# Where a Strassen sum is kept, where two halves of a weight tile lie, and ScalarE's order between two stages

## The chip, the cores and the metric

The kernel runs on one core of a Trainium2 chip. The metric is the device time of one execution in microseconds. The core's engines work side by side, each through its own list of instructions in order: TensorE (matmul, "PE", its weight loads "PEld"), VectorE ("DVE"), ScalarE ("ACT"), GpSimd ("POOL") and SyncE ("SP", which issues DMAs; GpSimd issues some too). They meet at semaphores: an instruction waits until the work that it depends on has been counted.

## The reference, cut to what matters

```python
def _attn_ref(q, k, v):                       # B=2, H=8, S=1152, D=64
    q_pool = q.reshape(B, H, S // 2, 2, D).mean(axis=3)
    scores = 1.0 / np.sqrt(D) * np.matmul(q_pool, k.transpose(0, 1, 3, 2))
    scores = scores - np.max(scores, axis=-1, keepdims=True)
    attn = np.exp(scores)
    attn = attn / (np.sum(attn, axis=-1, keepdims=True) + 1e-09)
    return np.matmul(attn, v)

def _moe_ref(x, domain_probs, w1, w2):        # x: 1152x512, 4 experts, F=1024
    p = domain_probs / (domain_probs.sum(-1, keepdims=True) + 1e-09)
    out = np.zeros((N, D))
    for e in range(E):
        h = np.maximum(x @ w1[e], 0.0)
        out += p[:, e:e + 1] * (h @ w2[e])
    return out
```

The attention output, as 1152 rows of 8 x 64 columns, is the `x` of the second function. Everything is fp32.

## The kernel before

**Stages.** Attention comes first: 8 pairs of heads, 9 tiles of 128 query rows each, 72 tiles in a row. Then 16 units of the expert layer, unit `u` being a quarter of one expert's hidden columns. Attention's tiles live in a pool `ap` that is closed at the end of the stage; a second pool `mp` lies over the same memory, and the first write to a tile of `mp` waits for the last users of every `ap` tile that it overlaps (`reuse_waits="tile"`). Tiles are laid out in the order in which they are made.

**fp32 in three products.** Each operand is split into a rounded half ("hi", z=0) and a remainder ("lo", z=1), and a product is hi·hi + hi·lo + lo·hi. The rounding is a ScalarE copy. The remainder is made by a subtraction on GpSimd or VectorE (`h_lo`, L715; `split_parts`, L496), or by rounding the negated value and adding the exact one by a DMA that accumulates (`h_add` L718, `w2_add` L742, `w1_add` L760).

**Strassen (Winograd form) in both layers.** One 2x2 block product takes 7 block products. The first layer's are `PRODS` (`mprod`, L139): they accumulate in three pairs of PSUM banks, CX, CY and CZ, and VectorE takes the sums u1, u2, C21, C22 and C12 out of them (`add_part`, L763). Bank pair CY is read three times while it grows: for u1, u2 and C21; in the first unit ScalarE also copies it once, as y7. After the relu these blocks give the operands of the second layer: S1 = C21 + C22 (GpSimd, L779), S2 = C11 - S1 and S3 = C11 - C21 (VectorE, L776), S4 = C12 + S2 (GpSimd `sum_s4`, L782). The second layer's products are P1 to P7 (`pprod`, L814), with weight blocks W and their sums T1 to T4 (`w2_sums`, L750), and VectorE adds them, weighted, into `acc` (L788, L790). `wide` (L826) does the rows left over.

**Where blocks are kept.** `UT` maps names to slots of the tile `xr`; several names share a slot, and the framework makes a write wait for all readers of what lay there. `hs` holds the split second-layer operands, `w2s` the split second-layer weights, for both z in one tile, `w1s` (in `kk`) the first-layer weights, `wf` and `w2f` their raw loads.

**Order.** Nothing is scheduled by a planner: each engine executes its instructions in the order of the code. Units overlap: the loop body for unit `u` interleaves the second layer of `u` with the first layer of `v = u + 1` and the weights of `w = u + 2`. On TensorE a unit is P5, P4, `mprod(v,2)`, `wide`, P3, `mprod(v,6)`, P2, then P1 of the next, `mprod(v,0)`, `mprod(v,1)`, P6, `mprod(v,3)`, P7, `mprod(v,5)`, `mprod(v,4)`. P2, P3 and P5 write CY, the others CO. On GpSimd `h_lo("S4")` stands behind `w1_add(w, 3, 7)`, late in the unit.

**The seam.** Between the last PV product (`PV_part`, L418, with `finish`, L455) and unit 0 the code of L844 to L894 makes the first operands: `w2_hi(0, "W")` and `w1_split(1, 0, 7, 1)` on ScalarE, `a11_hi`, the four roundings in `late` (S2, S1, A22, S4 of the last head pair's columns) with the copy of y7 between them.

Of the kernel before, what the change touches and what calls it, by code (L numbers as in the profile page):

```python
# [8 lines left out]
F32 = mybir.dt.float32  # L9
F32R = mybir.dt.float32r  # L10
# [7 lines left out]
def attention_moe_kernel(ctx, tc, q, k, v, probs, w1, w2, out):  # L18
    nc = tc.nc
    B, H, S, D = q.shape  # L20
    NT, DM = out.shape
    E, _, FF = w1.shape
    P = 128
    HALF = 64
    NPAIR = H // 2
    KT = S // P
# [75 lines left out]
    def flat(t):  # L102
        return t.rearrange("p o k f -> p (o k f)")
# [18 lines left out]
    def load_w2(u):  # L122
        if u < NU:
            e, j = divmod(u, 4)
            nc.sync.dma_start(w2f, w2[e].rearrange("(s j p) d -> j p s d", s=2, p=P)[j])

    UT = {n: xr[:, k, o * HT:(o + 1) * HT] for n, k, o in (
        ("m1", 0, 0), ("u1", 0, 1), ("u2", 2, 0), ("y7", 2, 1), ("C21", 1, 0), ("C22", 1, 1), ("S1", 3, 0), ("C12", 3, 1))}
    UT |= {"S2": UT["y7"], "S3": UT["u2"], "S4": UT["C21"]}
    UV = {n: t.rearrange("p (c x) -> p c x", c=2) for n, t in UT.items()}  # L130

    PRODS = [("X", "A11", "B11"), ("Y", "S2", "T2"), ("X", "A12", "B21"), ("Y", "S3", "T3"),
# [19 lines left out]
    with ExitStack() as actx:  # L152
        ap = actx.enter_context(tc.tile_pool(name="ap", bufs=1))

        vn = [ap.tile([P, 2, KT, D], F32, name=f"vn{i}") for i in range(2)]
        sx = [ap.tile([P, S], F32, name=f"sx{i}") for i in range(3)]
        raw = ap.tile([P, 7 * P], F32, name="raw")
        GW = [256, 320]
        aT = [ap.tile([P, 2, KT, w], F32, name=f"aT{i}") for i, w in enumerate(GW)]
        rb = [ap.tile([P, w], F32, name=f"rb{i}") for i, w in enumerate(GW)]  # L160
        spread = ap.tile([P, 4 * HALF], F32, name="spread")
        mn = [ap.tile([P, 1], F32, name=f"mn{i}") for i in range(3)]
# [246 lines left out]
        def PV_part(n, grp, k0, k1):  # L409
# [4 lines left out]
            po = opt[0]  # L414
            w = GW[grp]
            for kt in range(k0, k1):
# [32 lines left out]
        def finish(n, grp, po):  # L449
            b, hp = pairs[n]  # L450
            w, kt = GW[grp], hp % 2
            c = slice(256 * grp, 256 * grp + w)
# [45 lines left out]
        late = []  # L498
# [90 lines left out]
        for g in range(NTL):  # L589
            n, i = divmod(g, 9)  # L590
# [95 lines left out]

        mp = ctx.enter_context(tc.tile_pool(name="mp", bufs=1, reuse_waits="tile"))
        w2t = mp.tile([P, 4, 256], F32, name="w2t")
        acc = mp.tile([P, NQT, DM], F32, name="acc")
        w2s = mp.tile([P, 2, 12, 256], F32R, name="w2s")  # L690
        hs = mp.tile([P, 2, 61, HALF], F32R, name="hs")

        HS = {"A11": (0, 9), "S1": (10, 8), "A12": (19, 9), "A22": (29, 8), "A21": (10, 8), "S2": (37, 8), "S3": (45, 8), "S4": (53, 8),
# [26 lines left out]
        def rows(t):  # L720
            return t.rearrange("p o f -> p (o f)")

        def wop(u, w, z, n=1):
            o = WT[w] if w[0] == "T" else 4 * (u % 2) + 2 * int(w[1] == "2") + int(w[2] == "2")
            return rows(w2s[:, z, o:o + n])

        def w2_part(u, name):
            if name == "W":
                return [wop(u, "W11", z, 4) for z in range(2)], w2f.rearrange("p s f -> p (s f)")
            a, n = name  # L730
            return [rows(w2s[:, z, 8 + a:8 + a + n]) for z in range(2)], rows(w2t[:, a:a + n])

        def w2_hi(u, name, neg=True):
            if u < NU:
                dst, src = w2_part(u, name)
                for z in range(1 + neg):
                    nc.scalar.activation(dst[z], src, AF.Copy, scale=-1.0 if z else 1.0)

        def w2_add(u, name):
            if u < NU:  # L740
                dst, src = w2_part(u, name)
                nc.gpsimd.dma_start(dst[1].bitcast(F32), src, accum_op=ALU.add)  # L742

        def w2_sums(parts):
            w = {f"W{s + 1}{d + 1}": w2f[:, s, d * 256:(d + 1) * 256] for s in range(2) for d in range(2)}
            w |= {n: w2t[:, o - 8] for n, o in WT.items()}
            for i in parts:
                o, x, y, op = (("T1", "W12", "W11", ALU.subtract), ("T2", "T1", "W22", ALU.subtract),
                               ("T3", "W22", "W12", ALU.subtract), ("T4", "W21", "T2", ALU.add))[i]
                nc.gpsimd.tensor_tensor(w[o], w[x], w[y], op)  # L750

        def w1_split(u, a, b, z0=0):
            if u < NU:
                for z in range(z0, 2):
                    nc.scalar.activation(
                        flat(w1s[u % 2][:, z, a:b]), flat(wf[:, a:b]), AF.Copy, scale=-1.0 if z else 1.0)

        def w1_add(u, a, b):
            if u < NU:
                nc.gpsimd.dma_start(flat(w1s[u % 2][:, 1, a:b]).bitcast(F32), flat(wf[:, a:b]), accum_op=ALU.add)  # L760
# [48 lines left out]
        def pprod(u, name, chain=CO):  # L809
            op, w, b, d, first = PR2[name]  # L810
            pc = [chain[:, i // 2, (i % 2) * 256:(i % 2) * 256 + 256] for i in range(4)]
            for i in range(4):
                for m, (x, y) in enumerate(TERMS):
                    nc.tensor.matmul(pc[i], cols(op, x, 2 * i), wop(u, w, y),  # L814
                                     start=(first == 1 and m == 0 and i % 2 == 0), stop=(m == 2), skip_group_check=True)
                for t in range(i - 1, i + 1) if i % 2 else ():
                    gated(u, 4 * b + t, 256 * d, 256 * d + 256, pc[t])

        def wide(u, idx, pc, c0=0, c1=DM):
            for sl in range(2):  # L820
                if idx == 8:
                    op, o = (("A11", 8), ("A12", 8))[sl]
                else:
                    op, o = (("A11", "A12"), ("A21", "A22"))[idx // 4][sl], 2 * (idx % 4)
                for m, (x, y) in enumerate(TERMS):
                    nc.tensor.matmul(pc, cols(op, x, o), wop(u, f"W{sl + 1}1", y, 2)[:, c0:c1],  # L826
                                     start=(sl + m == 0), stop=(sl + m == 3), skip_group_check=True)
            gated(u, idx, c0, c1, pc)
            if u == NU - 1:
                store(idx, c0, c1)  # L830
# [4 lines left out]
        def mprod(u, p, kts=(0, 1)):  # L835
            n = PRODS[p][0]
            for kt in kts:
                product(u, p, kt, chains[n], (u, n) not in begun)
            begun.add((u, n))

        def copy_m1():
            nc.scalar.activation(UV["m1"], CX[:, :, :CW], AF.Copy)

        w2_hi(0, "W")  # L844
        w2_sums((0, 1))
        w2_add(0, "W")
        w2_sums((2, 3))
        load_w2(1)
        w1_split(1, 0, 7, 1)
        w1_add(1, 0, 7)  # L850
        load_w1(2)
        a11_hi()
        begun.add((0, "X"))
        mprod(0, 3)
        for p in late[:2]:
            p[0]()
        nc.scalar.activation(UV["y7"], CY[:, :, :CW], AF.Copy)  # L857
        mprod(0, 4, (0,))
        for p in late[2:]:
            p[0]()  # L860
        mprod(0, 1, (0,))
        for p in late:
# [1 line left out]
        mprod(0, 1, (1,))  # L864
        w2_hi(0, (0, 4), False)
        w2t_lo, w2t_src = w2_part(0, (0, 4))
        for c in range(2):
            cs = slice(c * 512, (c + 1) * 512)
# [148 lines left out]
```

## Time and profile before

| | us |
|---|---|
| median of 3 runs (638.51 to 639.1) | 638.57 |
| the profiled execution | 639.26 |
| its span | 637.5 |
| TensorE busy | 599.0 (94%) |
| weight loads busy | 530.7 (83%) |
| VectorE busy | 458.8 (72%) |
| GpSimd busy | 423.3 (66%) |
| ScalarE busy | 399.1 (63%) |

Attention runs to about 236 us in the span, the units from there to the end. In a timeline each line is a run of equal instructions: when the first began, how long until the last ended, engine, source line, operation, what it writes and reads, how many, and in brackets how long the engine had been idle before and which instruction ended that. Matmuls overlap a little, and their ends are modelled. Idle time of an engine costs nothing by itself; it matters where another engine waits for what comes late.

### The profile page before, as it was taken

The numbers are of one execution on the slowest core, as the hardware profiler recorded it, in microseconds if no ns is written. First come the engines' busy times: TensorE is split into PE (matmuls) and PEld (weight loads), VectorE is DVE, ScalarE is ACT, GpSimd is POOL, SyncE is SP. The second block draws the span as 40 slices with busy tenths as digits, with TensorE's granted clock in tenths as the row PEclk, the third lists the DMA queues.
The fourth block names the chain that finished last, engine by engine and source line by source line (L and its number), as shares of the span: only waits on it lengthen the run. The fifth ranks groups of instructions, "written<-read, shape, count | busy, mean of one in ns | idle before, by whom it ended". The sixth has DMA issues, their size and how long they took to land. (4 is left out here: it accounts for less than half of the span.)

```text
span 637.5 us, 14430 instructions
## 1 busy us (share of the span) xinstructions
PE 599.0 (94%) x5585; PEld 530.7 (83%) x5585; DVE 458.8 (72%) x903; ACT 399.1 (63%) x611; POOL 423.3 (66%) x534
## 2 busy tenths in 40 slices
PE   7999999999999998699999999999999999999997
PEld 6777777777777768598998988988988988988996
DVE  6778878777777765477677686786776776776774
ACT  5766777767767747556566666656756746746630
POOL 4746536455454966777977977977877977877620
PEclk9999999999999998899999999999999999999999
DMA  4877466484744207749569669579578587587415
GB/s 149 195 209 197 113 161 138 124 200 126 174 100 113 67 2 156 132 112 212 101 133 195 121 136 204 106 146 191 108 156 174 113 169 146 133 178 135 97 34 149
DMA packets 54180, 89.38 MB, mean 140 GB/s; under 512 B 4704, under 2 KB 28640, under 8 KB 54112
## 3 DMA queue, kind: packets, MB, share of 16 engines
q0 software_dynamic: 12672, 38.34, 34.0%
q1 hardware_dynamic: 40560, 48.94, 28.4%
q10 hardware_dynamic: 880, 1.18, 0.5%
q8 instruction: 44, 0.72, 0.5%
q14 instruction: 24, 0.20, 0.1%
HBM read 30.97 MB, written 2.36 MB: 52 GB/s over the span
## 5 line engine op out<-in xcount | busy, mean ns | idle before, releaser
L790 DVE SCALAR_TENSOR_TENSOR acc<-banks,pw,acc 128x256 f32<-128x256 f32 (+2 forms) x429 | 182.1, 488 | 13.9 <-PE banks L826 7.0
L814 PE MATMUL banks<-w2s,hs 128*128 128x256 f32 x1260 | 166.9, 286 | 24.8 <-DVE xr L763 24.8
L814 PEld LDWEIGHTS banks<-w2s,hs 128*128 128x128 f32 x1260 | 159.7, 193 | 29.7 <-DVE xr L763 28.2
L383 DVE TENSOR_SCALAR_CACHE_REDUCE sx<-banks 128x1152 f32<-128x1152 f32 x72 | 97.7, 1357 | 42.2 <-PE banks L372 19.1
L763 DVE TENSOR_TENSOR xr<-banks,xr 128x576 f32<-128x576 f32 x79 | 58.4, 754 | 90.0 <-POOL hs L715 44.3
L715 POOL TENSOR_TENSOR hs<-xr,hs 128x512 fp32r<-128x512 f32 (+2 forms) x79 | 95.9, 1232 | 25.4 <-ACT hs L712 13.8
L389 ACT ACTIVATE sx<-sx,mn 128x1152 f32<-128x1152 f32 x72 | 90.6, 1258 | 19.9 <-DVE sx L383 19.8
L766 ACT ACTIVATE xr<-xr 128x576 f32<-128x576 f32 x48 | 32.7, 681 | 106.8 <-DVE xr L763 106.8
L712 ACT ACTIVATE hs<-xr 128x512 fp32r<-128x512 f32 (+3 forms) x109 | 76.0, 725 | 21.2 <-DVE xr L776 18.7
L418 PE MATMUL banks<-aT,vn 128*64 128x320 f32 (+1 forms) x576 | 85.5, 418 | 0.0
L139 PE MATMUL banks<-xb,kk 128*128 128x288 f32 x480 | 77.5, 297 | 3.3 <-ACT xr L857 3.0
L139 PE MATMUL banks<-q2all,kk 128*128 128x288 f32 x448 | 76.1, 299 | 0.0
L139 PEld LDWEIGHTS banks<-xb,kk 128*128 128x128 f32 x480 | 68.5, 191 | 4.2 <-ACT xr L857 3.2
L405 ACT ACTIVATE aT<-banks 128x640 f32<-128x640 f32 x72 | 50.5, 702 | 30.4 <-PE banks L215 30.2
L139 PEld LDWEIGHTS banks<-q2all,kk 128*128 128x128 f32 x448 | 65.5, 191 | 0.0
L372 PEld LDWEIGHTS banks<-kk,q2all 64*128 64x128 f32 x504 | 54.5, 186 | 12.0 <-DVE sx L383 6.1
L372 PE MATMUL banks<-kk,q2all 64*128 64x512 f32 (+1 forms) x504 | 63.2, 365 | 0.5 <-DVE sx L383 0.5
L215 PEld LDWEIGHTS banks<-ident,sx 64*128 64x128 f32 x1296 | 54.4, 139 | 6.2 <-issue 2.7
L215 PE MATMUL banks<-ident,sx 64*128 64x64 f32 x1296 | 57.9, 225 | 1.3 <-ACT raw L238 0.5
L139 PE MATMUL banks<-xa,kk 128*128 128x288 f32 x384 | 56.9, 297 | 0.0
L742 POOL DMA_DIRECT2D w2s<-w2t x28 | 26.1, 933 | 46.1 <-issue 43.9
L98 POOL TENSOR_TENSOR kq<-kq 128x256 f32<-128x256 f32 x64 | 50.8, 870 | 6.4 <-DMA kq<-in_moe_w_dram 5.2
(120 smaller groups left out, 865.7 us busy)
## 6 DMA issues: line engine op xcount, KB each, us to landing
hs<-xr POOLq DMA_DIRECT2D x15, 576.0 KB, 4.9
kq<-in_moe_w_dram SPq DMA_DIRECT2D x64, 128.0 KB, 5.8
qsf<-in_moe_w_dram SPq DMA_DIRECT2D x16, 512.0 KB, 6.2
w2s<-qsf POOLq DMA_DIRECT2D x16, 512.0 KB, 5.0
q2all<-q2all SPq DMA_DIRECT2D x28, 256.0 KB, 4.1
kk<-kq POOLq DMA_DIRECT2D x14, 512.0 KB, 6.8
w2s<-w2t POOLq DMA_DIRECT2D x28, 256.0 KB, 4.9
kk<-kq POOLq DMA_DIRECT2D x14, 384.0 KB, 4.2
```

The lines of the kernel that those rows point to most:

```text
L98: nc.gpsimd.tensor_tensor(g(o), g(a), g(b), ALU.subtract)
L139: nc.tensor.matmul(chain[:, c, :CW], w1s[u % 2][:, a, WI[wo], kt, :], xop(xo, z, kt)[:, c * CW:(c + 1) * CW], start=(first and kt == 0 and ...
L215: nc.tensor.transpose(pt[:, a, j, :], src[r], ident[r, r])
L372: mm = nc.tensor.matmul(sp[:, cs[c]], q2[n % 2][r, zq, h, ts_], src[n % 2][r, zk, cs[c]], start=(zq + zk == 0), stop=(zq == 1), skip_group ...
L383: nc.vector.tensor_scalar(sx[g % 3].rearrange("p (c x) -> p c x", c=3), spt.pop(g), -INV, None, ALU.mult, ALU.min, accum_out=mn[g % 3])
L389: nc.scalar.activation(sx[g % 3], sx[g % 3], AF.Exp, bias=mn[g % 3], scale=-1.0, accum_out=sums[n % 2][:, i:i + 1])
L418: nc.tensor.matmul(po[h * HALF:(h + 1) * HALF, :w], vn[n % 2][:, h, kt, :], aT[grp][:, h, kt, :], start=(kt == 0), stop=(kt == KT - 1))
L712: nc.scalar.activation(hop(op, z), raw_of(op), AF.Copy, scale=-1.0 if z else 1.0)
L715: nc.gpsimd.tensor_tensor(hop(op, 1), raw_of(op), hop(op, 0).bitcast(F32), ALU.subtract)
L763: nc.vector.tensor_tensor(UV[name], chain[:, :, :CW], UV[part], ALU.add)
L790: nc.vector.scalar_tensor_tensor(ac, src, pw[:, idx, e:e + 1], ac, ALU.mult, ALU.add)
L814: nc.tensor.matmul(pc[i], cols(op, x, 2 * i), wop(u, w, y), start=(first == 1 and m == 0 and i % 2 == 0), stop=(m == 2), skip_group_check= ...
```

## The change

Three edits. S4 is formed in the slot of S2 (`y7`'s), in place, and no longer in the slot of C21. The split second-layer weights `w2s` become two tiles, `w2s0` (hi) and `w2s1` (lo), made before `acc`, and the order of attention's tiles in memory is changed: by their sizes `w2s0` lies over `vn0`, `sx0`, `sx1` and `raw`, `w2s1` over `raw`, `sx2` and `aT0`, `acc` over `aT0` and `aT1`, `hs` over `aT1`, `vn1`, `rb0`, `rb1` and the small tiles behind them. Before, `w2s` lay over `sx2`, `raw`, `aT0` and the start of `aT1`. At the seam `w1_split(1, 0, 7, 1)` goes ahead of `w2_hi(0, "W")` on ScalarE, and one rounding of `late`, not two, goes ahead of the copy of y7.

```diff
--- before.py
+++ after.py
@@ -126,7 +126,7 @@
 
     UT = {n: xr[:, k, o * HT:(o + 1) * HT] for n, k, o in (
         ("m1", 0, 0), ("u1", 0, 1), ("u2", 2, 0), ("y7", 2, 1), ("C21", 1, 0), ("C22", 1, 1), ("S1", 3, 0), ("C12", 3, 1))}
-    UT |= {"S2": UT["y7"], "S3": UT["u2"], "S4": UT["C21"]}
+    UT |= {"S2": UT["y7"], "S3": UT["u2"], "S4": UT["y7"]}
     UV = {n: t.rearrange("p (c x) -> p c x", c=2) for n, t in UT.items()}
 
     PRODS = [("X", "A11", "B11"), ("Y", "S2", "T2"), ("X", "A12", "B21"), ("Y", "S3", "T3"),
@@ -152,11 +152,13 @@
     with ExitStack() as actx:
         ap = actx.enter_context(tc.tile_pool(name="ap", bufs=1))
 
-        vn = [ap.tile([P, 2, KT, D], F32, name=f"vn{i}") for i in range(2)]
-        sx = [ap.tile([P, S], F32, name=f"sx{i}") for i in range(3)]
+        GW = [256, 320]
+        vn = [ap.tile([P, 2, KT, D], F32, name="vn0")]
+        sx = [ap.tile([P, S], F32, name=f"sx{i}") for i in range(2)]
         raw = ap.tile([P, 7 * P], F32, name="raw")
-        GW = [256, 320]
+        sx.append(ap.tile([P, S], F32, name="sx2"))
         aT = [ap.tile([P, 2, KT, w], F32, name=f"aT{i}") for i, w in enumerate(GW)]
+        vn.append(ap.tile([P, 2, KT, D], F32, name="vn1"))
         rb = [ap.tile([P, w], F32, name=f"rb{i}") for i, w in enumerate(GW)]
         spread = ap.tile([P, 4 * HALF], F32, name="spread")
         mn = [ap.tile([P, 1], F32, name=f"mn{i}") for i in range(3)]
@@ -686,8 +688,8 @@
 
         mp = ctx.enter_context(tc.tile_pool(name="mp", bufs=1, reuse_waits="tile"))
         w2t = mp.tile([P, 4, 256], F32, name="w2t")
+        w2s = [mp.tile([P, 12, 256], F32R, name=f"w2s{z}") for z in range(2)]
         acc = mp.tile([P, NQT, DM], F32, name="acc")
-        w2s = mp.tile([P, 2, 12, 256], F32R, name="w2s")
         hs = mp.tile([P, 2, 61, HALF], F32R, name="hs")
 
         HS = {"A11": (0, 9), "S1": (10, 8), "A12": (19, 9), "A22": (29, 8), "A21": (10, 8), "S2": (37, 8), "S3": (45, 8), "S4": (53, 8),
@@ -722,13 +724,13 @@
 
         def wop(u, w, z, n=1):
             o = WT[w] if w[0] == "T" else 4 * (u % 2) + 2 * int(w[1] == "2") + int(w[2] == "2")
-            return rows(w2s[:, z, o:o + n])
+            return rows(w2s[z][:, o:o + n])
 
         def w2_part(u, name):
             if name == "W":
                 return [wop(u, "W11", z, 4) for z in range(2)], w2f.rearrange("p s f -> p (s f)")
             a, n = name
-            return [rows(w2s[:, z, 8 + a:8 + a + n]) for z in range(2)], rows(w2t[:, a:a + n])
+            return [rows(w2s[z][:, 8 + a:8 + a + n]) for z in range(2)], rows(w2t[:, a:a + n])
 
         def w2_hi(u, name, neg=True):
             if u < NU:
@@ -841,22 +843,22 @@
         def copy_m1():
             nc.scalar.activation(UV["m1"], CX[:, :, :CW], AF.Copy)
 
+        w1_split(1, 0, 7, 1)
         w2_hi(0, "W")
         w2_sums((0, 1))
         w2_add(0, "W")
         w2_sums((2, 3))
         load_w2(1)
-        w1_split(1, 0, 7, 1)
         w1_add(1, 0, 7)
         load_w1(2)
         a11_hi()
         begun.add((0, "X"))
         mprod(0, 3)
-        for p in late[:2]:
+        for p in late[:1]:
             p[0]()
         nc.scalar.activation(UV["y7"], CY[:, :, :CW], AF.Copy)
         mprod(0, 4, (0,))
-        for p in late[2:]:
+        for p in late[1:]:
             p[0]()
         mprod(0, 1, (0,))
         for p in late:
```

The engines' lists differ in ScalarE's at the seam alone; elsewhere only waits and the tile names do. Below stands ScalarE's list at the seam before, each row with the semaphores that it waits for (`w2s<-qsf` is `w2_hi(0, "W")`, `kk_75<-kq` is `w1_split`, `hs<-banks` is `a11_hi`, `q2all<-xr` are the roundings of `late`, `xr<-banks` is the copy of y7).

```order
L737 ACTIVATE w2s<-qsf 128x1024 [waits DMAHW4_49,PE_49,Activation_49]
L737 ACTIVATE w2s<-qsf 128x1024
L755 ACTIVATE kk_75<-kq 128x1792 [waits DMAHW5_49,DMAHW6_49,DMAHW3_49,DMAHW7_49,DMAHW0_49,Pool_49]
L769 ACTIVATE hs<-banks 128x576 [waits DVE_49,Pool_49]
L495 ACTIVATE q2all<-xr 128x320 [waits DVE_49] x2
L857 ACTIVATE xr<-banks 128x576 [waits PE_49]
L495 ACTIVATE q2all<-xr 128x320
L495 ACTIVATE q2all<-xr 128x320 [waits DVE_49]
L737 ACTIVATE w2s<-w2t 128x1024 [waits Pool_49]
```

And the same place now (`w2s_3456` is `w2s0`, `w2s_3457` is `w2s1`).

```order
L757 ACTIVATE kk_75<-kq 128x1792 [waits DMAHW5_49,DMAHW4_49,DMAHW6_49,DMAHW3_49,DMAHW7_49,DMAHW0_49,Pool_49]
L739 ACTIVATE w2s_3456<-qsf 128x1024 [waits DMAHW4_49,Activation_49]
L739 ACTIVATE w2s_3457<-qsf 128x1024 [waits PE_49,Activation_49]
L771 ACTIVATE hs<-banks 128x576 [waits DVE_49,DMAHW3_49,Activation_49,Pool_49]
L497 ACTIVATE q2all<-xr 128x320 [waits DVE_49]
L859 ACTIVATE xr<-banks 128x576 [waits PE_49]
L497 ACTIVATE q2all<-xr 128x320 [waits DVE_49]
L497 ACTIVATE q2all<-xr 128x320
L497 ACTIVATE q2all<-xr 128x320 [waits DVE_49]
L739 ACTIVATE w2s_3456<-w2t 128x1024 [waits Pool_49]
```

The split of w1 stands first, the first rounding of W has lost its wait for TensorE (the second has one, for the PV products that read `aT0`), and the copy of y7 is the second row behind `a11_hi`, not the third.

VectorE's list has the same instructions in the same order. Before, at the place in a middle unit where P7's last sums (L790) are followed by C21 (the first L763), C22 (the second) and P5's first sum:

```order
L790 SCALAR_TENSOR_TENSOR acc<-banks,pw,acc 128x256 [waits PE_49]
L790 SCALAR_TENSOR_TENSOR acc<-banks,pw,acc 128x256
L763 TENSOR_TENSOR xr<-banks,xr 128x576 [waits PE_49,Activation_49,Pool_49]
L763 TENSOR_TENSOR xr<-banks,xr 128x576 [waits DVE_49,PE_49]
L790 SCALAR_TENSOR_TENSOR acc<-banks,pw,acc 128x256 [waits DVE_49,PE_49]
```

Now:

```order
L792 SCALAR_TENSOR_TENSOR acc<-banks,pw,acc 128x256 [waits PE_49]
L792 SCALAR_TENSOR_TENSOR acc<-banks,pw,acc 128x256
L765 TENSOR_TENSOR xr<-banks,xr 128x576 [waits PE_49,Pool_49]
L765 TENSOR_TENSOR xr<-banks,xr 128x576 [waits DVE_49,PE_49,Pool_49]
L792 SCALAR_TENSOR_TENSOR acc<-banks,pw,acc 128x256 [waits DVE_49,PE_49]
```

C21's row has lost its wait for ScalarE (`h_hi("S4")`) and keeps one for GpSimd; C22's row has one for GpSimd that it did not have.

## Rows read from the trace of the kernel before

**Rows 1.** The page, slices of the span; granted TensorE clock in tenths.

```profile
PEclk9999999999999998899999999999999999999999
```

**Rows 2.** Waits of the whole span: who waited for whom; us, times, longest.

```profile
PEld banks L814 <- DVE xr L763: 28.2, 14, 6.0
PE banks L814 <- DVE xr L763: 24.8, 14, 5.8
```

**Rows 3.** Timeline, TensorE, a middle unit; start, us, work, [idle before].

```profile
441.04 3.14 PE L814 MATMUL banks<-w2s,hs 128*128 128x256 f32 x24 [1.46 <-DVE xr L763]
...
450.02 3.04 PE L814 MATMUL banks<-w2s,hs 128*128 128x256 f32 x24
...
462.95 0.96 PE L139 MATMUL banks<-q2all,kk 128*128 128x288 f32 x6
465.37 3.14 PE L814 MATMUL banks<-w2s,hs 128*128 128x256 f32 x24 [1.46 <-DVE xr L763]
```

**Rows 4.** Timeline, TensorE's weight loads, the same unit.

```profile
465.37 2.81 PEld L814 LDWEIGHTS banks<-w2s,hs 128*128 128x128 f32 x23 [1.70 <-DVE xr L763]
```

**Rows 5.** Timeline, VectorE, the same unit.

```profile
445.89 1.42 DVE L776 SCALAR_TENSOR_TENSOR xr<-banks,xr 128x576 f32<-128x576 f32 x2 [0.61 <-PE banks L139]
...
448.77 1.65 DVE L790 SCALAR_TENSOR_TENSOR acc<-banks,pw,acc 128x256 f32<-128x256 f32 x4
...
464.56 1.42 DVE L763 TENSOR_TENSOR xr<-banks,xr 128x576 f32<-128x576 f32 x2 [2.86 <-POOL hs L715]
```

**Rows 6.** Timeline, GpSimd, the same unit.

```profile
443.88 1.74 POOL L779 TENSOR_TENSOR xr<-xr 128x576 f32<-128x576 f32 x1
...
447.40 4.24 POOL L715 TENSOR_TENSOR hs<-xr,hs 128x512 fp32r<-128x512 f32 x4 [0.94 <-DVE xr L776]
...
462.66 1.87 POOL L715 TENSOR_TENSOR hs<-xr,hs 128x512 fp32r<-128x512 f32 x1
```

**Rows 7.** Timeline, TensorE, the seam and unit 0.

```profile
242.08 1.06 PE L139 MATMUL banks<-xb,kk 128*128 128x288 f32 x6 [2.95 <-ACT xr L857]
...
249.27 1.60 PE L814 MATMUL banks<-w2s,hs 128*128 128x256 f32 x12
...
261.33 0.96 PE L139 MATMUL banks<-q2all,kk 128*128 128x288 f32 x6
268.06 5.49 PE L814 MATMUL banks<-w2s,hs 128*128 128x256 f32 x24 [5.77 <-DVE xr L763]
```

**Rows 8.** Timeline, ScalarE, the seam.

```profile
236.64 2.01 ACT L737 ACTIVATE w2s<-qsf 128x1024 fp32r<-128x1024 f32 x2 [4.13 <-PE banks L418]
...
241.39 0.64 ACT L857 ACTIVATE xr<-banks 128x576 f32<-128x576 f32 x1
```

**Rows 9.** Timeline, VectorE, the seam.

```profile
230.48 0.83 DVE L469 TENSOR_TENSOR xr<-xr 128x256 f32<-128x256 f32 x1
...
236.59 0.49 DVE L455 TENSOR_TENSOR xr<-banks,rb 128x320 f32<-128x320 f32 x1 [0.79 <-PE banks L418]
...
237.53 0.48 DVE L469 TENSOR_TENSOR xr<-xr 128x320 f32<-128x320 f32 x1
```

**Rows 10.** Timeline, GpSimd, the seam and unit 0.

```profile
230.23 2.84 POOL L113 TENSOR_SCALAR kk<-kq 128x512 fp32r<-128x512 f32 x4
...
241.15 1.14 POOL L760 DMA_DIRECT2D kk<-kq  x1
...
258.09 0.87 POOL L718 DMA_DIRECT2D hs<-xr  x1
...
265.35 1.86 POOL L715 TENSOR_TENSOR hs<-xr,hs 128x512 fp32r<-128x512 f32 x1
```

**Rows 11.** Busy time by stretch: length, engines, granted clock, DMA share.

```profile
244.00:246.00 2.00, 2.00 (x10) 2.00 (x9) 0.99 (x2) 0.00 (x0) 2.00 (x2) 0.50 0.93 183
```

**Rows 12.** DMA issues, 225 to 275: count, size, us to landing.

```profile
kk<-kq POOLq DMA_DIRECT2D x1, 896.0 KB, 8.2
hs<-xr POOLq DMA_DIRECT2D x1, 576.0 KB, 5.7
```

## The prediction, made before the changed kernel was timed

> **What bounds the kernel now.** I read the page's clock line first, then the waits in total, then the timeline engine by engine: one middle unit, and the seam where attention ends. TensorE has the full clock but for two slices at the seam [rows 1]. Its waits are nearly all of one kind: the second-layer product P5 (L814) waits for VectorE's L763, 14 times, 24.8 us; by weight loads 28.2 us [rows 2]. One was 5.77 long [rows 7]; the other 13 are alike.
>
> In a middle unit TensorE goes from P5 to P5 in 465.37 - 441.04 = 24.33 us and stands 1.46 idle before P5 [rows 3]. P5 writes bank pair CY, which `add_part("C21", CY, "m1")` must read first; that sum sat 2.86 us behind GpSimd's `hs L715` [rows 5], which is `h_lo("S4")`, 462.66 to 464.53 [rows 6]. It waits because S4 lies in C21's slot: the new C21 may not be written before the old S4's remainder is taken. TensorE finished the product that feeds C21 six matmuls earlier. GpSimd's chain thus holds every unit.
>
> At the seam ScalarE stood idle 4.13 us before `w2_hi(0,"W")` (236.64), which waited for the last PV product because `w2s` lay over `aT1` [rows 8]. Behind it queue `w1_split`, `a11_hi`, two roundings and the copy of y7 (241.39), for which TensorE waited 2.95 us [rows 7, 8]. After that pause the granted clock was 0.50, the lower of its two levels (1.2 of 2.4 GHz), in 244 to 246 [rows 11], and P5 of unit 0 took 5.49 us for 24 matmuls behind its 5.77 pause, against 3.14 in a middle unit [rows 3, 7].
>
> **The change part by part.** *S4 in S2's slot.* No instruction is added. C21's sum still waits for GpSimd in the new order, but the last GpSimd reader of its slot is now `h_lo("L")` of the unit before, inside the group of four from 447.40 to 451.64, 10 us early [rows 6]. C22's new wait is for `h_lo("A22")` of that group, and ScalarE's roundings of T2 to T4, which now name GpSimd, wait for `w2_sums`, done before `h_lo("S4")` starts. S2's next writer, `c11_less("S2")`, comes 4.85 us behind P5 (445.89) [rows 5], when `h_lo("S4")` has ended; and `sum_s4` writes over an S2 that GpSimd itself has read before. So the pause goes. What is late next? The four things P5 needs (S1's halves, T1's halves, bank CY, C21's sum) are all ready before the product ahead of it ends. I price a pause by the weight loads: 1.70 [rows 4], against 1.46 by matmul idle [rows 3]; the difference is the overlap of one matmul with the next, lost at each pause. 12 units (P5 of units 2 to 13) x 1.70 = 20.4 us; by 1.46 it would be 17.5.
>
> A page bears on these two numbers. The Trainium skill's "Perfetto Trace Analysis", Per-engine timelines (Tensor Engine Instruction), says that the end of a matmul in the trace is computed from its size, only the start observed. By that rule idle between end and start is not a measure, and start-to-start or the weight loads are, which here gives 20.4 and not 17.5; the rows alone cannot say which end is true, and I keep both for the range.
>
> Does GpSimd keep up? From S2's sum (445.89) to `h_lo("S2")` 1.51 us, from there to the end of `h_lo("S4")` 17.13, a DMA issue 0.6, `sum_s1` 1.74 [rows 5, 6]: 20.98 until the next S2 sum can start. The new unit is 24.33 - 1.70 = 22.63, so 1.65 us is left.
>
> *The seam: ScalarE.* `w2s0` now lies over `vn0`, `sx0`, `sx1`, `raw`, `w2s1` over `raw`, `sx2`, `aT0`, all last read before 230, so nothing holds ScalarE at 232.51 (236.64 - 4.13). `w1_split` has 1792 columns; at W's two roundings' 2.01 for 2048 that is 1.7, to 234.2, and W's own end at 236.1. `a11_hi` still waits for `finish` (236.59 + 0.49) [rows 9], since `hs` lies over `aT1`, `vn1` and `rb1`: 237.1 to 237.8. One rounding of 320 columns follows (0.4, scaled from 0.64 for 576 columns [rows 8]), then y7, now second instead of third. Its product ended six matmuls before 242.08 - 2.95 = 239.13, at 238.35; so the copy runs 238.45 to 239.09 and TensorE resumes at 239.14 instead of 242.08: 2.94 us. From there to P1 of unit 0 (249.27) stand 42 matmuls; at the full clock (3.14 / 24 = 0.13 each, with one refill) 5.7 us, they took 7.19: 1.49 come back. New on the path: the three roundings now behind y7 and VectorE's remainders delay the sum u2 to about 241.75, 0.3 behind TensorE. GpSimd's `w2_sums((2, 3))` moves 2.5 us up, beside VectorE's sums from 237.1. When GpSimd worked beside it (L113 from 230.23, [rows 10]) L469 took 0.83 for 256 columns, alone 0.48 for 320 [rows 9]: 0.2 more. P1 comes 2.94 + 1.49 - 0.5 = 3.9 us earlier; bounds 2.95 (the pause alone) and 4.4 (no new wait).
>
> A page speaks against this step. The Trainium skill's "SBUF — State Buffer", SBUF: two separate sides, says that a VectorE operation with two SBUF inputs and a GpSimd operation that reads SBUF take turns, each blocking the other whole. The two L469 rows agree. By the rule, with both of GpSimd's sums in the way, u2 would lose up to about 0.8 instead of 0.2, and P1 would gain 3.3; it touches no sum in a middle unit, whose VectorE work reads PSUM and one SBUF tile.
>
> *DMAs that move.* `w1_add(1)` goes out 2.5 us earlier (241.15), its first reader behind P1 3.9 earlier; it landed 8.2 after issue [rows 10, 12], at 249.35, just behind P1's start, and P1's 12 matmuls cover about 1.5. That leaves 0.1: I take 0, bound 0.5. The loads of SP behind it come earlier too, and delay nothing.
>
> *Unit 0.* P5 would start 3.9 earlier than 261.33 + 0.80, at 258.2. Its third matmul reads S1's remainder, which `h_add` brings: issued at 258.09, landing 5.7 us later [rows 10, 12]; both 3.9 earlier, that is 259.9. So a wait hidden before appears: 259.9 - 258.2 - 0.26 + 0.2 for the refill = 1.6 us (0 if it lands in 4.1, 4.1 if it needs 8.2). P5 starts in effect at 259.8 against 268.06: 8.3. The 2.35 of slow clock (5.49 - 3.14) comes back too, since 1.46 pauses in 13 units left the clock at full [rows 1, 3]. Then GpSimd: `h_lo("S4")` ends at 267.21 - 3.9 = 263.3 [rows 10], a DMA issue and `sum_s1` later S1 is ready at 265.65, while S2's sum wants it 4.85 behind P5, at 264.65. That 1.0 passes through VectorE to P3's gated sums, whose first half ends 448.77 + 0.82, 0.43 before P2 (450.02) needs the bank [rows 3, 5]: 0.6 lost (0 to 1.0). P5 of unit 1: 8.3 + 2.35 + 1.70 - 0.6 = 11.7 us earlier.
>
> *Sum.* 11.7 + 20.4 = 32.1. The profiled execution took 639.26 (span 637.5 and 1.76 around it), 0.69 above the median 638.57: 607.2 there, 606.5 as median.
>
> **Rivals.** *GpSimd becomes the bound.* With 1.65 us left in its loop, `sum_s1` behind ScalarE's relu of C22 could be late in each unit as in unit 0. Decides when the loop passes 22.63. For it: its waits in the loop are on ScalarE and VectorE, which move too. Against: 1.65 is more than any one of them. Price 0.6 to 1.0 in 12 units, about 9.5: 616. *The wait stays*: if the region that C21's sum waits for still covers `h_lo("S4")`, only the seam is won, 3.9: 634.7. Against: the reader list in the code. *Slower, by the clock.* TensorE without pauses might be granted less. It decides if half clock falls on more than 64 us of the units (32.1 lost); with a quarter of some 340 us at half clock, +42: 649. Against: in attention, without such pauses, the clock stood at full [rows 1]; the two dips follow pauses, not work.
>
> **How the numbers follow.** Forecast 0.80, GpSimd bound 0.10, wait stays 0.04, clock 0.02, and 0.04 for more than I count (below 603.5). The forecast's own ends: all new waits zero and 4.4 at the seam gives 34.8, 603.8; pauses at 1.46 (-3.1), landing 8.2 (-2.5) and the lock (-0.6) give 25.9, 612.7. Range 603.5 to 612.5. A measurement here can tell 0.2%, 1.3 us, from no change; every case but the clock and a broken forecast is beyond that: faster 0.96, same 0.01, slower 0.03.
>
> **What would show it.** P5 to P5 of 22.6 in a middle unit; no wait of L763 on `hs L715`, and in the waits by engine none of L814 on L763; y7's copy ending near 239.1 and P1 of unit 0 near 245.4; one wait of some 1.5 us in P5 of unit 0 for a DMA into `hs`; no 0.50 clock from 240 to 280. Wrong if P5 to P5 stays above 23.2, if a new wait on GpSimd shows in each unit, or if the clock dips in the units.

## The result, and the profile after

The changed kernel took 608.42 us (median of 4 runs, 607.84 to 609.02) against 638.74 for the kernel before beside it: ratio 0.9525, 95% interval 0.9508 to 0.9541. The profiled execution took 607.84, with a span of 606.1 against 637.5. Measured again in a later set of runs it took 606.84 (4 runs, 606.53 to 609.61), ratio 0.9501 (0.9477 to 0.9525). The forecast was 606.5, range 603.5 to 612.5.

The page of the changed kernel: busy time by engine, and the granted clock by slice, the line that answers to [rows 1].

```profile
PE 591.5 (98%) x5585; PEld 526.4 (87%) x5585; DVE 459.7 (76%) x903; ACT 399.0 (66%) x611; POOL 423.1 (70%) x534
PEclk9999999999999999999999999999999999999999
```

Its waits, the largest of TensorE's: who waited for whom, us in total, times, longest. They answer to [rows 2].

```profile
PE banks L816 <- DMA hs<-xr: 2.3, 1, 2.3
PE banks L521 <- DVE xa L39: 1.2, 1, 1.2
PE banks L139 <- ACT xr L859: 1.1, 1, 1.1
```

The 14 waits of the second-layer product for VectorE are gone. One wait of it is left, for a DMA, in unit 0; and one at the seam for the copy of y7.

A middle unit on TensorE (timeline: start, us, work), as in [rows 3]: P5, P2, the product ahead of P5, P5.

```profile
397.42 3.04 PE L816 MATMUL banks<-w2s,hs 128*128 128x256 f32 x24
...
406.30 3.04 PE L816 MATMUL banks<-w2s,hs 128*128 128x256 f32 x24
...
419.23 0.97 PE L139 MATMUL banks<-q2all,kk 128*128 128x288 f32 x6
420.03 3.04 PE L816 MATMUL banks<-w2s,hs 128*128 128x256 f32 x24
```

P5 to P5 is 420.03 - 397.42 = 22.61 (24.33 before), and no idle time stands before it. VectorE's and GpSimd's timelines of the same unit show why, the rows that answer to [rows 5, 6]:

```profile
418.70 0.76 DVE L765 TENSOR_TENSOR xr<-banks,xr 128x576 f32<-128x576 f32 x1 [0.71 <-POOL w2t L752]
420.29 0.76 DVE L765 TENSOR_TENSOR xr<-banks,xr 128x576 f32<-128x576 f32 x1 [0.83 <-PE banks L139]
```

```profile
399.75 1.74 POOL L781 TENSOR_TENSOR xr<-xr 128x576 f32<-128x576 f32 x1
...
403.68 4.22 POOL L717 TENSOR_TENSOR hs<-xr,hs 128x512 fp32r<-128x512 f32 x4 [0.98 <-DVE xr L778]
...
418.92 1.88 POOL L717 TENSOR_TENSOR hs<-xr,hs 128x512 fp32r<-128x512 f32 x1
421.75 0.87 POOL L744 DMA_DIRECT2D w2s<-w2t  x1 [0.95 <-POOL hs L717]
```

C21's sum (the first L765) starts at 418.70, before `h_lo("S4")` at 418.92 has even begun; it used to wait for that instruction's end. The bracket names a sum of w2's blocks on GpSimd, which ended 0.06 us before. The product that feeds C21 ended just as near (418.59), so the rows do not say which of the two it waited for; TensorE lost nothing by it.

The seam and unit 0 on TensorE, as in [rows 7]: the first product behind attention, the one that waits for y7, P1, P5 (two matmuls, then the others), P2.

```profile
236.41 1.06 PE L139 MATMUL banks<-xb,kk 128*128 128x288 f32 x6
...
240.20 1.06 PE L139 MATMUL banks<-xb,kk 128*128 128x288 f32 x6 [1.14 <-ACT xr L859]
...
246.27 1.60 PE L816 MATMUL banks<-w2s,hs 128*128 128x256 f32 x12
...
259.14 0.40 PE L816 MATMUL banks<-w2s,hs 128*128 128x256 f32 x2
261.88 2.90 PE L816 MATMUL banks<-w2s,hs 128*128 128x256 f32 x22 [2.34 <-DMA hs<-xr]
...
270.62 3.04 PE L816 MATMUL banks<-w2s,hs 128*128 128x256 f32 x24
```

TensorE resumes at 240.20 and not at 239.14 as forecast. ScalarE, VectorE and GpSimd there, the rows that answer to [rows 8 to 10]:

```profile
233.94 1.99 ACT L739 ACTIVATE w2s<-qsf 128x1024 fp32r<-128x1024 f32 x2
237.19 0.65 ACT L771 ACTIVATE hs<-banks 128x576 fp32r<-128x576 f32 x1 [1.26 <-DVE xr L457]
239.14 0.47 ACT L497 ACTIVATE q2all<-xr 128x320 fp32r<-128x320 f32 x1 [1.30 <-DVE xr L483]
239.52 0.63 ACT L859 ACTIVATE xr<-banks 128x576 f32<-128x576 f32 x1
```

```profile
233.20 0.95 DVE L498 TENSOR_TENSOR kk<-xr,q2all 128x256 fp32r<-128x256 f32 x1
...
236.53 0.49 DVE L457 TENSOR_TENSOR xr<-banks,rb 128x320 f32<-128x320 f32 x1 [0.78 <-PE banks L420]
237.06 2.05 DVE L483 TENSOR_TENSOR xr<-xr 128x320 f32<-128x320 f32 x1
239.03 0.48 DVE L471 TENSOR_TENSOR xr<-xr 128x320 f32<-128x320 f32 x1
```

```profile
232.98 0.89 POOL L752 TENSOR_TENSOR w2t<-qsf 128x256 f32<-128x256 f32 x1
233.95 0.79 POOL L752 TENSOR_TENSOR w2t<-w2t,qsf 128x256 f32<-128x256 f32 x1
...
237.06 1.01 POOL L752 TENSOR_TENSOR w2t<-qsf 128x256 f32<-128x256 f32 x1
237.76 0.99 POOL L752 TENSOR_TENSOR w2t<-qsf,w2t 128x256 f32<-128x256 f32 x1
238.44 1.14 POOL L762 DMA_DIRECT2D kk<-kq  x1
```

VectorE's L483 started in the same moment as the first of GpSimd's two sums and ended 0.36 us behind the second (239.11 against 238.75). It took 2.05 us, and L471 behind it, with the same width, 0.48. ScalarE's rounding (L497, which stood idle 1.30 us for L483) and the copy of y7 (L859) come behind it. It is not always two that hold VectorE up: L498 at 233.20 ended at 234.15, while the second sum of the pair before (233.95 to 234.74) was still running. The pair at 237.06 stands right behind a DMA issue of GpSimd, and its two records overlap; what decides between the cases is not shown.

### The profile page after: what moved, and what is told of

It reads as the page before. It is cut to its first block, busy times and chain, and to the rows that moved or that the text cites. A ratio compares the mean times of both kernels' runs of the same rounds, so it can differ in the third digit from the quotient of the medians.

```text
span 606.1 us, 14475 instructions
## 1 busy us (share of the span) xinstructions
PE 591.5 (98%) x5585; PEld 526.4 (87%) x5585; DVE 459.7 (76%) x903; ACT 399.0 (66%) x611; POOL 423.1 (70%) x534
## 4 chain that ended last, share of the span: by engine, by line
PE 93%; DMA 2%; POOL 2%; DVE 1%; ACT 1%; issue 1%; SPq 0%; POOLq 0%; DVEq 0%; ACTq 0%
PE banks L139 28%; PE banks L816 24%; PE banks L420 13%; PE banks L217 9%; PE banks L374 9%; PE banks L828 6%; PE banks L356 4%; DMA hs<-xr 1%; DMA kq<-in_k_dram 1%; DVE sx L385 1%; POOL hs L717 0%; ACT sx L391 0%; ACT aT L407 0%; DVE xr L483 0%; POOL kk L260 0%
## 5 line engine op out<-in xcount | busy, mean ns | idle before, releaser
L816 PE MATMUL banks<-w2s,hs 128*128 128x256 f32 x1260 | 163.3, 283 | 2.3 <-DMA hs<-xr 2.3
L816 PEld LDWEIGHTS banks<-w2s,hs 128*128 128x128 f32 x1260 | 158.0, 191 | 3.9 <-DMA hs<-xr 2.5
L765 DVE TENSOR_TENSOR xr<-banks,xr 128x576 f32<-128x576 f32 x79 | 59.7, 756 | 66.0 <-PE banks L139 45.7
L407 ACT ACTIVATE aT<-banks 128x640 f32<-128x640 f32 x72 | 50.5, 701 | 30.3 <-PE banks L217 30.1
L139 PEld LDWEIGHTS banks<-xa,kk 128*128 128x128 f32 x384 | 52.4, 189 | 0.5 <-issue 0.4
```

Of the source, the lines that this page charges most:

```text
L139: nc.tensor.matmul(chain[:, c, :CW], w1s[u % 2][:, a, WI[wo], kt, :], xop(xo, z, kt)[:, c * CW:(c + 1) * CW], start=(first and kt == 0 and ...
L765: nc.vector.tensor_tensor(UV[name], chain[:, :, :CW], UV[part], ALU.add)
L816: nc.tensor.matmul(pc[i], cols(op, x, 2 * i), wop(u, w, y), start=(first == 1 and m == 0 and i % 2 == 0), stop=(m == 2), skip_group_check= ...
```

## The experiments

Times of one kernel vary by up to 4.7 us between the runs of one set (the kernel before: 637.08 to 641.82), so for each kernel the profiled run is also read by three stretches of TensorE's timeline: from its first product behind attention to P1 of unit 0, to P2 of unit 0, and from there to the end of the span. Worked out from the starts, for the kernel before from 236.48, 249.27 and 279.68:

```
kernel        median (runs)  ratio to before (95%)     to P1   to P2   P2 to end
before        638.7  (4)     1                         12.79   43.20   357.8
after         608.42 (4)     0.9525 (0.9508, 0.9541)    9.86   34.21   335.5
s4_only       610.12 (4)     0.9547 (0.9529, 0.9564)   12.79   37.02   335.2
seam_only     635.83 (6)     0.9949 (0.9935, 0.9963)    9.85   39.61   357.5
sums_first    606.75 (5)     0.9494 (0.9478, 0.9510)    8.63   32.77   335.8
w1_back       607.19 (4)     0.9503 (0.9486, 0.9521)    8.65   34.33   335.6
hadd_early    607.82 (5)     0.9501 (0.9481, 0.9521)    8.65   32.74   335.6
s1_on_dve     605.14 (4)     0.9458 (0.9439, 0.9477)    8.66   31.18   335.7
pad2          609.34 (4)     0.9518 (0.9495, 0.9542)    9.85   35.58   335.7
pad6          620.80 (4)     0.9702 (0.9681, 0.9723)    9.86   33.95   347.7
tiles_only    607.00 (5)     0.9495 (0.9477, 0.9514)    8.79   34.70   335.7
after_2       606.84 (4)     0.9501 (0.9477, 0.9525)    9.87   35.54   335.7
best_2        605.04 (4)     0.9465 (0.9448, 0.9481)    8.65   31.19   335.9
```

**s4_only**, the slot alone:

```diff
-    UT |= {"S2": UT["y7"], "S3": UT["u2"], "S4": UT["C21"]}
+    UT |= {"S2": UT["y7"], "S3": UT["u2"], "S4": UT["y7"]}
```

> The kernel before with one line changed: S4 takes S2's slot (y7) instead of C21's. The tiles of w2's halves and ScalarE's order at the seam stay as before. Theory (the slot alone removes the pause of each unit): P5 to P5 22.6 us instead of 24.33 in a middle unit and no wait of C21's sum on GpSimd; P1 of unit 0 still at 249.3 behind a pause of about 2.9 us; in unit 0 the wait for C21's sum goes and a wait of about 1.4 us for the DMA into hs appears. That gives 20.4 (12 units) and about 8 in unit 0, together some 28.5: about 610. Rival (the seam's edits are needed for GpSimd to catch up, so that without them each unit keeps part of its pause): about 625.

610.12. TensorE's timeline: the pause for y7, P1 and P5 of unit 0, two P5 of the middle.

```profile
242.01 1.06 PE L139 MATMUL banks<-xb,kk 128*128 128x288 f32 x6 [2.95 <-ACT xr L857]
...
249.20 1.60 PE L814 MATMUL banks<-w2s,hs 128*128 128x256 f32 x12
...
264.69 2.90 PE L814 MATMUL banks<-w2s,hs 128*128 128x256 f32 x22 [2.23 <-DMA hs<-xr]
...
400.23 3.04 PE L814 MATMUL banks<-w2s,hs 128*128 128x256 f32 x24
...
422.85 2.32 PE L814 MATMUL banks<-w2s,hs 128*128 128x256 f32 x18
```

P5 to P5 is 22.62 with the seam untouched. By the medians one line of code gives 28.7 of the 30.3 us, and the rival falls: GpSimd needs none of the seam's edits to keep up. Only the DMA's wait is larger than I expected, 2.23 instead of 1.4.

**seam_only**, the change without that line:

```diff
-    UT |= {"S2": UT["y7"], "S3": UT["u2"], "S4": UT["y7"]}
+    UT |= {"S2": UT["y7"], "S3": UT["u2"], "S4": UT["C21"]}
```

> The changed kernel with S4 put back into C21's slot, so that only the two tiles of w2's halves and ScalarE's order at the seam remain of the change. Theory: P1 of unit 0 stays 3.0 us earlier than in the kernel before, the pause of about 1.7 us before each P5 is back: about 635.6. Rival (the tiles and the order bring most of the gain, by GpSimd's and ScalarE's earlier start): about 615.

635.83, and the pause is back in each unit (14 waits of P5 for VectorE, 24.5 us):

```profile
240.77 1.06 PE L139 MATMUL banks<-xb,kk 128*128 128x288 f32 x6 [1.14 <-ACT xr L859]
...
389.22 3.14 PE L816 MATMUL banks<-w2s,hs 128*128 128x256 f32 x24 [1.44 <-DVE xr L765]
```

The seam is worth 2.9 us by itself at P1 (12.79 to 9.85) and 3.6 at P2 of unit 0. With the slot moved as well, 2.8 of it arrives at P2 in the first profile of the changed kernel (37.02 to 34.21) and 1.5 in the second (35.54).

**sums_first**, GpSimd's second pair of sums before a DMA issue, so that they end before L483:

```diff
         w2_sums((0, 1))
-        w2_add(0, "W")
         w2_sums((2, 3))
+        w2_add(0, "W")
```

> The changed kernel with one call moved: GpSimd forms the second pair of w2's sums before the DMA issue of w2_add for unit 0, so they run at about 234.7 to 236.4, before VectorE's 320-column sum L483 at 237.06. Theory (the two engines hold each other up: L483 took 2.05 us beside the two GpSimd sums, 0.49 without them): L483 is back at about 0.5, the copy of y7 ends about 1 to 1.5 us earlier, TensorE's wait at 240.2 goes, P1 of unit 0 at about 245.0 instead of 246.27; total 606.5 to 607.2 (part of it may be given back where P5 of unit 0 waits for its DMA). Rival (L483 is long because of something else that runs then, a transfer or ScalarE): L483 stays at about 2 us and the time at 608.4.

Its profile, VectorE and then TensorE (P1, P5 behind its first two matmuls, P2):

```profile
237.77 0.49 DVE L483 TENSOR_TENSOR xr<-xr 128x320 f32<-128x320 f32 x1
```

```profile
245.76 1.60 PE L816 MATMUL banks<-w2s,hs 128*128 128x256 f32 x12
...
259.59 2.89 PE L816 MATMUL banks<-w2s,hs 128*128 128x256 f32 x22 [0.58 <-DMA hs<-xr]
...
269.90 3.21 PE L816 MATMUL banks<-w2s,hs 128*128 128x256 f32 x24 [1.42 <-DVE acc L792]
```

L483 is back at 0.49, TensorE's wait for y7 is gone, and P1 stands 8.63 behind the first product instead of 9.86. It was GpSimd's two sums that had held L483 up, and not a DMA issue alone: here L483 ran beside one (L762, 237.75 to 238.90). (Attention ended 0.7 later in this run, so the starts themselves don't compare.) At P2 a new wait of 1.42 shows: VectorE stood for S1, which GpSimd forms. The median of 606.75 lies 1.7 us under the changed kernel's first median and 0.1 under its second; the time alone shows no gain.

**w1_back**, `w1_split` behind the load of w2 as before:

```diff
-        w1_split(1, 0, 7, 1)
         w2_hi(0, "W")
...
         load_w2(1)
+        w1_split(1, 0, 7, 1)
```

> The changed kernel with w1_split put back behind the load of w2, as before, so that w2's roundings are ScalarE's first work at the seam again; GpSimd's sums of w2 then start about 1.7 us earlier and end at about 237.3. Theory (it was moving w1_split to the front that put GpSimd's sums beside VectorE's L483): L483 at most 0.8 us instead of 2.05, the copy of y7 about 1 us earlier, total about 607.2. Rival (w1_split in front is what lets ScalarE be done in time; behind w2's roundings it pushes a11_hi and the copy of y7 back): P1 of unit 0 not earlier, total 608.4 to 609.5.

607.19. L483 takes 0.49 and P1 comes 8.65 behind the first product. So moving `w1_split` to the front put the sums beside L483, and cost 1.2 us at P1. P5 of unit 0:

```profile
260.45 4.41 PE L816 MATMUL banks<-w2s,hs 128*128 128x256 f32 x22 [2.17 <-DMA hs<-xr]
```

The DMA's wait of 2.17 is followed by 22 matmuls in 4.41 us, 1.5 more than the 2.90 in the first profile of the changed kernel, at a granted clock of 0.63 and 0.52 in 260 to 264: the seam's gain is given back there.

**hadd_early** adds to w1_back, in unit 0, an earlier issue of that DMA:

```diff
+        if seam:
+            h_add("S1A12")
+            h_lo("A22")
         w1_sums(w, (0, 1))
-        h_add("S1A12")
+        if not seam:
+            h_add("S1A12")
```

(`h_lo("A22")` went just ahead of the loop before.)

> The kernel w1_back (the changed kernel with w1_split behind the load of w2) with one more edit, in unit 0 only: GpSimd issues h_add, the DMA into hs that P5 of unit 0 waits for, ahead of h_lo of A22 and w1_sums, some 2.7 us earlier. In w1_back that DMA held P5 for 2.17 us, after which 22 matmuls took 4.41, and P2 of unit 0 began at 270.70. Theory (two things bound unit 0, and behind the DMA stands GpSimd's chain to S1): the DMA's wait and the slow matmuls go, but S1 still comes from GpSimd at 265.3, and P2 begins 3.8 us behind it (in sums_first S1 at 266.07, P2 at 269.90), at 269.1, behind a wait of about 2.3 us: 1.6 us gained, 605.6. Rival (the DMA alone bounds unit 0): P2 at 266.8, 3.9 us gained, 603.3.

Its timelines, TensorE and VectorE:

```profile
257.80 3.04 PE L816 MATMUL banks<-w2s,hs 128*128 128x256 f32 x24
...
269.02 3.20 PE L816 MATMUL banks<-w2s,hs 128*128 128x256 f32 x24 [2.18 <-DVE acc L792]
```

```profile
265.23 1.42 DVE L778 SCALAR_TENSOR_TENSOR xr<-banks,xr 128x576 f32<-128x576 f32 x2 [3.28 <-POOL xr L781]
```

P5 runs without a wait at 257.80, and P2 stands at 269.02 (forecast 269.1) behind a wait of 2.18: VectorE waits 3.28 for GpSimd's `sum_s1`. The wait has moved, as the first theory had it; the DMA-alone rival (266.8) falls. The time shows none of it: 607.82 instead of 605.6. The profiled run took 606.44, the other four 607.8 to 609.2, at mean granted clocks of 0.992 to 0.996 against 0.998. That these lost it at half clock behind the 2.18 pause is likely from the clocks, but no trace of them exists.

**s1_on_dve** adds to hadd_early: S1 of unit 0 on VectorE.

```diff
+        if seam:
+            nc.vector.tensor_tensor(UT["S1"], UT["C21"], UT["C22"], ALU.add)
         if not last:
             c11_less("S2", "S1")
```

(GpSimd's `sum_s1` is left out in that unit.)

> hadd_early with S1 of unit 0 formed by VectorE, just ahead of the sum into S2, instead of by GpSimd (sum_s1); the other units keep it on GpSimd. Theory (GpSimd's chain to S1 is what still bounds unit 0): no wait before P2 of unit 0, which begins at about 266.8 to 267.0, and 603.3 to 603.7. Rival (something else holds P2, or the sum on VectorE, which reads two SBUF tiles beside GpSimd's remainder of S4, is held up as L483 was): as hadd_early, or up to 1 us above it.

605.14, all four runs within 0.32. VectorE and TensorE:

```profile
262.05 1.65 DVE L961 TENSOR_TENSOR xr<-xr 128x576 f32<-128x576 f32 x1
```

```profile
267.64 3.21 PE L816 MATMUL banks<-w2s,hs 128*128 128x256 f32 x24 [0.61 <-DVE acc L792]
```

P2's wait falls from 2.18 to 0.61, so GpSimd's chain to S1 did bound unit 0. The rest is most likely the hold-up again, though no run takes it away: the sum took 1.65 beside GpSimd's remainder of S4 (261.17 to 263.08), where L882 of the same form took 0.75, and ended 0.62 behind it. best_2 repeats it (1.68, and a wait of 0.64). The miss of 1.5 us has two parts. The 0.61 is one. The other is my reckoning: I took 3.9 us, read from a w1_back profile that held the slow 4.41 us, off w1_back's median, which holds that in only some of its runs. From the profiled run itself (608.16) the 34.33 - 31.18 = 3.15 gives 605.0.

**pad2 and pad6**, idle work on GpSimd in each unit but the first (k = 2, 6):

```diff
+        for _ in range(0 if seam else k):
+            nc.gpsimd.tensor_tensor(ident, ident, ident, ALU.mult)
         h_lo("S4")
```

> The changed kernel with 2 idle products of a 128x128 tile on GpSimd, about 0.4 to 0.45 us each, just ahead of the remainder of S4 in every unit but unit 0. Theory (GpSimd's loop has 1.65 us left in a unit): about 0.9 us of it is used, P5 to P5 stays 22.6, the time 608.4. Rival (GpSimd bounds the units already): about 0.9 in 12 units, 619.

> As pad2 with 6 such products, about 2.5 to 2.7 us. Theory (1.65 us left in a unit): the loop is 0.9 to 1.05 us too long, P5 to P5 23.5 to 23.7, in 12 units 11 to 13 more: 619 to 621. Rival (GpSimd has far more to give, since its idle stretches in a unit sum to 2.3 us and what follows it can wait): no change, 608.4.

pad2: 335.7 from P2 to the end, as in the changed kernel; its 609.34 is more than the changed kernel's medians, and the excess lies ahead of P2 (35.58), where the granted clock was 0.50 in 264 to 266. pad6: 620.8. Its middle unit on GpSimd, VectorE and TensorE (two P2):

```profile
425.05 3.41 POOL L931 TENSOR_TENSOR ident<-ident 128x128 f32<-128x128 f32 x6
428.41 1.30 POOL L717 TENSOR_TENSOR hs<-xr,hs 128x512 fp32r<-128x512 f32 x1
```

```profile
432.02 1.42 DVE L778 SCALAR_TENSOR_TENSOR xr<-banks,xr 128x576 f32<-128x576 f32 x2 [1.70 <-POOL xr L781]
```

```profile
412.27 3.21 PE L816 MATMUL banks<-w2s,hs 128*128 128x256 f32 x24 [0.61 <-DVE acc L792]
...
435.82 3.21 PE L816 MATMUL banks<-w2s,hs 128*128 128x256 f32 x24 [0.61 <-DVE acc L792]
```

The unit is 23.55 long, 0.94 over 22.61. GpSimd had 3.41 more to do, less 0.58 by which the remainder behind it was shorter (1.30 against 1.88): 2.83 - 0.94 = 1.9 us were free, where the prediction counted 1.65. (The remainder is shorter because a DMA issue no longer stands right ahead of it, see the last section.) The bound comes where it said, at S2's sum behind `sum_s1`. Both rivals fall.

**tiles_only**, w1_back with two roundings ahead of y7's copy, as before:

```diff
-        for p in late[:1]:
+        for p in late[:2]:
```

(The loop behind the copy takes `late[2:]`.)

> The changed kernel with ScalarE's order at the seam as before: w1_split behind the load of w2, and two roundings of attention ahead of the copy of y7. Left of the change are S4 in S2's slot and the two tiles of w2's halves over buffers that are read last early. Theory (the tiles alone free ScalarE at the seam; the order moves the copy of y7 by one rounding): the copy ends about 0.5 us later than in w1_back, 239.4, TensorE waits about 0.5, P1 of unit 0 at 245.5 against 245.0: 607.2 to 607.7, that is below the changed kernel's 608.4, since L483 is not held up here. Rival (ScalarE's order is what brings the seam's 3 us): y7 as late as in s4_only, a wait of some 2.9 us, about 610.

607.0, P1 at 8.79 against 8.65. Above s4_only it changes only the tiles: 4.0 us at P1, more than the whole change brings there. ScalarE's new order is worth 0.14 by y7's place and costs 1.2 by `w1_split`'s.

**after_2 and best_2**: the changed kernel and s1_on_dve again, side by side.

> The changed kernel again, on the chip of the next run, for a direct comparison: 608.4.

> s1_on_dve again, beside the changed kernel on one chip: 605.1, some 3.3 us below it, if what it gained holds against the changed kernel; 607 or more if part of the gain lay in the other chip.

606.84 and 605.04. s1_on_dve is faster than the changed kernel: its eight runs lie between 604.97 and 605.32, the changed kernel's eight between 606.53 and 609.61. The gap of medians here is 1.8 us, not 3.3, and the intervals of the two ratios overlap a little. The profile of after_2, P5 of unit 0, and a window of it (length; busy us of PE, PEld, DVE, ACT, POOL; granted clock; DMA share, GB/s):

```profile
261.84 4.27 PE L816 MATMUL banks<-w2s,hs 128*128 128x256 f32 x22 [2.16 <-DMA hs<-xr]
```

```profile
264.00:266.00 2.00, 2.00 (x11) 2.00 (x11) 1.34 (x4) 0.31 (x2) 2.00 (x3) 0.50 1.04 187
```

The same window in the first profile of the changed kernel:

```profile
264.00:266.00 2.00, 2.00 (x18) 2.00 (x17) 1.89 (x5) 1.23 (x4) 2.00 (x3) 1.00 1.06 192
```

It is the same program. In the first profile the 22 matmuls behind a pause of 2.34 took 2.90 us at full clock; here, behind 2.16, they take 4.27, and the clock stands at its lower level (1.2 of 2.4 GHz) in 264 to 266. That is 1.37 of the 1.77 us between the two profiled runs.

## Why the prediction was right

The mechanism and nearly all of the size held; two costs, one at the seam and one in unit 0, were put too small.

*The pause in each unit.* Forecast 20.4. P5 of unit 1 to P5 of unit 13 was 587.35 - 295.03 = 292.32 before and is 555.71 - 284.35 = 271.36: 20.96 gained, 1.75 a unit. Of the two prices, that by weight loads (1.70, [rows 4]) was right and that by matmul idle (1.46, [rows 3]) too low. The Trainium skill's "Perfetto Trace Analysis", Per-engine timelines (Tensor Engine Instruction), says that the end of a matmul in the trace is a model and not a measurement. The 1.75, which is read from starts alone, agrees. That heading takes in weight loads too, so the page does not choose between the two prices, though the prediction let it; the starts of the two traces do. s4_only shows that the slot alone does it.

*GpSimd's margin.* 1.65 forecast, about 1.9 by pad6; its loop bounds nothing from unit 1 on.

*The seam.* Forecast 3.9 us at P1, measured 3.0: TensorE resumed 1.9 us earlier (242.08 to 240.20) and not 2.94. The step that failed is the cost of GpSimd's `w2_sums((2, 3))` beside VectorE's sums, which the prediction put at 0.2, from an L469 that was 0.83 long, and only on the way to u2. L483 took 1.56 more than alone, and it passed this on by another way: ScalarE's rounding waits for L483, and the copy of y7 behind that rounding ended at 240.15 instead of 239.09. sums_first and w1_back, each by moving other instructions apart, bring L483 back to 0.49 and P1 1.2 us forward. The Trainium skill's "SBUF — State Buffer", SBUF: two separate sides, says that these two operations exclude each other, and the rows agree: L483 finished only behind the second of GpSimd's sums, L961 only behind the remainder. My estimate by that rule came nearer at P1 (3.3), but it too let the hold-up reach u2 alone, and with 0.8 at most.

*Unit 0.* The new wait for `h_add`'s DMA was forecast at 1.6 and cost 261.88 - 0.26 - 259.14 = 2.5: the transfer landed 6.8 us after its issue (255.08 to 261.88) where it had been 5.7 [rows 12]; the median of the 15 such transfers in the trace is 4.8. The 0.6 us for a late S1 was not lost, since the longer DMA wait covered it; in sums_first and hadd_early, where that wait is shorter or gone, it shows (1.42, 2.18). P2 of unit 0 comes 9.06 earlier and P5 of unit 1 10.68, forecast 11.7: the seam and the DMA took 0.9 each off, and the S1 that cost nothing gave 0.6 back, the clock 0.3.

*The clock.* "No 0.50 clock from 240 to 280" holds in the first profile and fails in after_2: the long pauses are gone, but behind the one left in unit 0 the clock fell at times: in after_2, w1_back, pad2 and tiles_only (pauses of 2.16 to 2.42), not in the first profile and s4_only (2.34, 2.23). The rival that TensorE would be granted less in the units falls: 300 to 600 shows full clock, and P2 to the end is 335.2 to 335.9 in the ten profiles with the slot and no more than pad2's padding.

*Sum.* 10.7 + 21.0, less 0.2 at the end, is the 31.4 by which the span fell; forecast 32.1. That it came so near is in part luck: the gain was forecast 0.6 us too low at the pauses and 0.6 at S1, and 0.9 too high both at the seam and at the DMA's wait. The medians fell by 30.3 in the first set and by 32.8 in the second. Why three of the four runs of after_2 lie at 606.5 to 606.9, below the profiled 607.84, is open: no trace of them exists.

## What to carry to other kernels

When one instruction in a loop waits for another engine each time, look first whose slot the result is written to: a reader of the old value, on a third engine, can be the whole wait, and here another slot cost nothing. Before moving work on GpSimd to another moment, look which two-input sums VectorE has there, follow what stands behind each of them, and let the upper bound of the hold-up be the whole of GpSimd's run of instructions (L483) and not one of them (L498). And where a wait is taken away, name the next chain behind it: in unit 0 y7, then the DMA, then S1 each held TensorE in turn, and edits that gained 1 to 2 us at one point showed no clear gain in the time until S1 was mended as well.

## What the runs showed of the hardware that was not expected

- VectorE's sum of two SBUF tiles was held for as long as GpSimd ran two of its own one behind the other: 2.05 us instead of 0.49 (320 columns), and 1.65 beside one (576 columns; L882, of the same form, took 0.75).
- The same program, with a pause of 2.2 to 2.3 us at the same place, kept the full clock in one execution and fell to half in another (22 matmuls in 2.90 and 4.27 us). s1_on_dve, whose longest pause there is 0.64, varied by 0.35 us over eight runs, the changed kernel by 3.1. The length of the pause does not sort the six profiles that have one before P5: 2.90 us behind 2.34 and 2.23, 3.93 to 4.41 behind 2.16, 2.17, 2.24 and 2.42.
- An instruction of GpSimd right behind one of its DMA issues is longer in the trace. The remainder `h_lo` (128x512) took 1.62 to 1.91 us at the 15 places of the changed kernel where an issue stands right ahead, and 1.28 to 1.30 at 5 single ones where none does; with the padding of pad2 and pad6 between the two, `h_lo("S4")` took 1.3.
- The same 576 KB transfer landed 6.6 to 6.8 us after its issue in after, after_2, w1_back and tiles_only, and 5.0 and 4.8 in sums_first and pad6, in whose profiles attention had ended some 0.7 us later; in seam_only, where it had ended 0.6 later, it took 6.5. What decides this stays open.
